# Windowed attention: one 144-column mask-and-exponential per score tile, 32-bit score products for eight units

## The chip, the cores and the metric

The kernel runs on one core of one Trainium2 chip. TensorE (PE in the profile) multiplies; VectorE (DVE), ScalarE (ACT) and GpSimd (POOL) do the rest; SyncE (SP) and ScalarE issue the transfers. The metric is the device time of one execution in microseconds, as the median of three runs.

## What is computed

Three stages follow each other: windowed attention with sink keys, a dense layer with SoLU and layer norm, and a layer of eight experts of which each token uses one. The change touches the attention and the loading of one weight.

```python
# attention, for 4 batches and 8 heads of 768 x 64; n_sink = 4, window = 128
scores = q @ k.T / sqrt(64)
keep = (key < n_sink) | ((0 <= query - key) & (query - key < window))
a = softmax(where(keep, scores, -1e9));  out = a @ v
# dense layer, 3072 tokens: x 512 -> 1024 -> 512
h = x @ w_in;  solu = h * softmax(h);  y = layernorm(solu) * g_ln @ w_out
# experts: e = argmax(y @ w_gate);  result = gate * relu(y @ w1[e]) @ w2[e]
```

## The kernel before

**Attention** works in 32 units of two heads and 384 queries. A unit has six score tiles (three blocks of 128 queries, two heads). A tile has 272 columns: the 128 keys of the block before, 16 sink keys, the 128 keys of the own block (for the first block of a sequence: own keys, sinks, 128 columns that the mask closes). `a_scores` makes the product in PSUM, DVE adds the mask and takes the row's extreme (line 220), ACT takes the exponential and its sum (222). After six tiles DVE adds the two 128-column parts (231: of a query, every key offset lies in one of the two blocks and is masked in the other), POOL scales by the sum (232, and 240 for the sinks). `a_trans` transposes on PE (270), and two masked copies on POOL (274, 276) part the two blocks again. `a_out` multiplies with the values (286, 292), and ACT and DVE split the result into a high and a low part (297, 298), the `xh`, `xl` of the dense layer.

**Scores in two ways.** The first three units (`NATP`) multiply in plain 32-bit: one product per tile on 64 partitions, the two heads on the two halves of the array (line 214). Later units use the faster reduced format, with the operands split into high and low parts (`a_split`): two roundings on ACT (179, 180), two subtractions on POOL (181, 182), nine transfers of SP per unit (187), and then two products of 128 partitions per tile (217, 218).

**Weights.** `w_in` and `w_out` come as 64-bit floats, in 16 chunks of 512 KB. `decode` waits for a transfer that ACT issues (315, three buffers), and works with three DVE operations (319, 321, 326), two of ACT (322, 324) and one of POOL (325); when 325 and 324 are done, the chunk's buffer is free. Its result lies in PSUM. `w_in` then takes one rounding and one subtraction (334, 335). `w_out` takes 363 and 364, a copy to SBUF on ACT (367), and the gate product: four transposes and four small products on PE (343, 351) with a copy between them (345).

**The dense layer** (`moe1`) has 24 tiles of 128 tokens; lines 421 to 423 are the first product (`h`), 491 to 493 the second (`x`). Tiles 3m to 3m+2 need the four units 4m to 4m+3. The experts follow.

**What sets the order.** Each engine runs its instructions in the order of the program. Generators write the work in a fixed interleaving (110 steps of attention with the 16 chunks among them, then both by shares), and a scheduler with its own table of durations reorders that at build time. PSUM has eight banks; attention has three of them (`PA`).

Of the kernel before, what the change touches and what calls it, by code (L numbers as in the profile page):

```python
# [8 lines left out]
F32 = mybir.dt.float32  # L9
F32R = mybir.dt.float32r  # L10
BF16 = mybir.dt.bfloat16
I32 = mybir.dt.int32
U32 = mybir.dt.uint32
AF = mybir.ActivationFunctionType
ALU = mybir.AluOpType
# [10 lines left out]
NEG = -8.0e9  # L26
# [3 lines left out]
NPT, XBUFS, QKB, PKB, VB = 2, 8, 2, 2, 2  # L30
WB, DB, EB, NXR, XGB = 3, 4, 2, 2, 6
PA = 3
NATP = 3
KLV = 2
LA = 2
TE = 18
# [8 lines left out]
E_MIN = struct.unpack("<f", struct.pack("<I", 897 << 20))[0]  # L45


def raw(ap):
    return ap.bitcast(F32)
# [3 lines left out]
def body(ctx, tc, a):  # L53
    nc = tc.nc
    V, A, G, T, SY = nc.vector, nc.scalar, nc.gpsimd, nc.tensor, nc.sync
# [20 lines left out]
    at = a_ctx.enter_context(tc.tile_pool(name="at", bufs=1, side="right"))  # L76

    def ps(name):
        if name in ATT:
            a_ = True  # L80
        elif name in MOE:
            a_ = False
        else:
            flip[0] += 1
            a_ = flip[0] % 8 < PA
        return ps_p.tile([128, 512], F32, tag="psa" if a_ else "psm", name=name, bufs=PA if a_ else 8 - PA)
# [7 lines left out]
                    pattern=[[-1, 128]], channel_multiplier=1)  # L94
# [19 lines left out]
    nsk, win = par[:, 0:1], par[:, 1:2]  # L114


    mkb = at.tile([128, 3, 272], BF16, name="mk")
    mk = at.tile([128, 3, 272], F32, tag="P", name="mkf", bufs=2)
    rel = at.tile([128, 3, 272], F32, tag="P", name="rel", bufs=2)
    mk = at.tile([128, 3, 272], F32, tag="P", name="mkf", bufs=2)  # L120
    kid = const.tile([128, 3, NS], F32, name="kid")
# [15 lines left out]
    def in_win(out, r, tmp):  # L137
# [5 lines left out]
    V.tensor_scalar(out=kid, in0=kid, scalar1=nsk, scalar2=None, op0=ALU.is_lt)  # L143
    V.scalar_tensor_tensor(out=mk[:, :, 128:144], in0=mk[:, :, 128:144], scalar=0.5, in1=kid, op0=ALU.is_lt,
                           op1=ALU.mult)
    V.tensor_scalar(out=mkb, in0=mk, scalar1=-1.0, scalar2=-NEG, op0=ALU.add, op1=ALU.mult)

# [3 lines left out]
    def unit(n):  # L153
        b, c = divmod(n, H)
        return b, c // 4, c % 4

    def a_load(n):
        b, hf, j = unit(n)
        nat = n < NATP
        qd = at.tile([128, 384], F32, tag="qA" if nat else "qd", name="qd", bufs=QKB)  # L160
# [39 lines left out]
    def a_scores(n, mid=()):  # L200

        b, hf, j = unit(n)
        P = at.tile([128, 2, 3, 272], F32, tag="P", name="P", bufs=2)
        mx = at.tile([128, 6], F32, tag="mx", name="mx", bufs=2)
        sm = at.tile([128, 6], F32, tag="sm", name="sm", bufs=2)
        for i in range(3):
            for r in range(2):
                rows = slice(64 * r, 64 * r + 64)
                s = ps("s")
                c0 = 144 * max(3 * hf + i - 1, 0) - KB[hf]  # L210
                qs, ks = slice(128 * i, 128 * i + 128), slice(c0, c0 + 272)
                if n < NATP:
                    q, k = qk_t[n][r]
                    T.matmul(s[:, 0:272], q[rows, qs], k[rows, ks], start=True, stop=True)
                else:
                    q, ql, k = qk_t[n][r]
                    T.matmul(s[:, 0:272], q[:, qs], k[:, ks], start=True, stop=False)  # L217
                    T.matmul(s[:, 0:272], ql[:, qs], k[:, ks], start=False, stop=True)  # L218
                cc = slice(3 * r + i, 3 * r + i + 1)
                V.tensor_tensor_reduce(out=P[:, r, i, :], in0=s[:, 0:272], in1=mkb[:, min(3 * hf + i, 2), :],  # L220
                                       scale=-0.125, scalar=3.0e38, op0=ALU.add, op1=ALU.min, accum_out=mx[:, cc])
                A.activation(out=P[:, r, i, :], in_=P[:, r, i, :], func=AF.Exp, scale=-1.0, bias=mx[:, cc],  # L222
                             accum_out=sm[:, cc])
                yield 0.45 if n < NATP else 0.23
            if i == 1:
                yield from mid
        P = P.rearrange("p r i c -> p (r i) c")
        V.tensor_scalar(out=sm, in0=sm, scalar1=1.0e-9, scalar2=None, op0=ALU.add)
        V.reciprocal(sm, sm)
        pk = at.tile([128, 6, 128], F32, tag="pk", name="pk", bufs=PKB)  # L230
        V.tensor_tensor(out=pk, in0=P[:, :, 0:128], in1=P[:, :, 144:272], op=ALU.add)
        G.tensor_tensor(out=pk, in0=pk, in1=sm.unsqueeze(2).to_broadcast([128, 6, 128]), op=ALU.mult)
        pk_t[n] = pk
        g = n % 2
        if g == 0:
            psk_t[n // 2] = at.tile([128, 3, 4, 2, NS], F32, tag="psk", name="psk")
        psk = psk_t[n // 2].rearrange("p i g a k -> p g i a k")[:, 2 * g:2 * g + 2]
        for r in range(2):
            rs = slice(3 * r, 3 * r + 3)
            G.tensor_tensor(out=psk[:, r], in0=P[:, rs, 128:144].unsqueeze(2).to_broadcast([128, 3, 2, NS]),  # L240
                            in1=sm[:, rs].unsqueeze(2).unsqueeze(3).to_broadcast([128, 3, 2, NS]), op=ALU.mult)
# [66 lines left out]
    def dec_tile(name):  # L308
        return dec_p[0].tile([128, 512], I32, tag="dec", name=name, bufs=DB)

    def decode(src):

        w = dec_p[0].tile([128, 512, 2], I32, tag="w64", name="w64", bufs=WB)
        with tc.issue_after(first_d.ins) if dec_p[0] is at else ExitStack():
            A.dma_start(out=w, in_=src)
        lo, hi = w[:, :, 0], w[:, :, 1]
        t = dec_tile("dec")
        t0 = ps("dt").bitcast(I32)
        V.tensor_scalar(out=t0, in0=hi, scalar1=0x07FFFFFF, scalar2=3, op0=ALU.bitwise_and,
                        op1=ALU.logical_shift_left)  # L320
        V.scalar_tensor_tensor(out=t, in0=hi, scalar=-0x40000000, in1=t0, op0=ALU.bitwise_and, op1=ALU.bitwise_or)
        A.activation(out=lo, in_=lo.bitcast(U32), func=AF.Copy, scale=2.0 ** -29)
        x = ps("dh")
        A.activation(out=x, in_=hi.bitcast(F32), func=AF.Abs)
        G.tensor_tensor(out=t, in0=t, in1=lo, op=ALU.add)
        V.scalar_tensor_tensor(out=x, in0=x, scalar=E_MIN, in1=t.bitcast(F32), op0=ALU.is_ge, op1=ALU.mult)
        return x

    def load_w_in():
        for k in range(4):  # L330
# [7 lines left out]
    def load_w_out():  # L338
        def logits(k, x):

            t = ps("wt")
            for d in range(4):
                T.transpose(t[:, 128 * d:128 * d + 128], x[:, 128 * d:128 * d + 128], ident)
            xt = dec_tile("xt").bitcast(F32).rearrange("p (a b) -> p a b", a=4)
            A.activation(out=xt, in_=t.rearrange("p (a b) -> p a b", a=4), func=AF.Copy)
            return k, xt

        def logits2(k, xt):
            t = ps("wt2")
            for d in range(4):  # L350
                T.matmul(t[:, 0:NE], xt[:, d, :], wg_sb[:, d, :], start=(d == 0), stop=(d == 3))
            wp = t[:, 0:NE]
            gk = g_sb[:, k:k + 1]
            V.tensor_scalar(out=woh[:, k, 0, 256:264], in0=wp, scalar1=gk, scalar2=None, op0=ALU.mult)
            V.scalar_tensor_tensor(out=wol[:, k, 0, 256:264], in0=wp, scalar=gk, in1=raw(woh)[:, k, 0, 256:264],
                                   op0=ALU.mult, op1=ALU.subtract)

        last = last2 = None
        for k in range(8):
            p = decode(a["w_out"].bitcast(I32)[128 * k:128 * k + 128, :])  # L360
            h_ = woh[:, k, :, 0:256]
            p2 = p.rearrange("p (a b) -> p a b", a=2)
            A.activation(out=h_, in_=p2, func=AF.Copy, scale=g_sb[:, k:k + 1])
            V.scalar_tensor_tensor(out=wol[:, k, :, 0:256], in0=p2, scalar=g_sb[:, k:k + 1], in1=raw(h_),
                                   op0=ALU.mult, op1=ALU.subtract)
            x = dec_tile("dec").bitcast(F32)
            A.activation(out=x, in_=p, func=AF.Copy)
            if last2:
                logits2(*last2)
                last2 = None  # L370
            if last:
                last2 = logits(*last)
            last = (k, x)
            yield 1.5
        logits2(*last2)
        logits2(*logits(*last))
# [4 lines left out]
                    channel_multiplier=-1)  # L381
# [704 lines left out]
    def attention():  # L1086
# [34 lines left out]
        for n in range(nu):  # L1121
            if n + 1 < nu:
                a_load(n + 1)
            if n:
                values(n - 1)
            yield from a_scores(n, sinks(n // 2 - 1))
            yield from finish(n, 0)
            if n + 1 < nu:
                a_split(n + 1)
            yield from finish(n, n - 1)  # L1130
# [144 lines left out]
```

## Time and profile before

| | us |
|---|---|
| Median of three runs | 839.44 (838.94 to 843.57) |
| The profiled execution | 844.13, span 842.4 |
| PE busy in the span | 786.0 (93%) |
| DVE, ACT, POOL busy | 495.4, 494.4, 385.4 |
| Mean granted TensorE clock | 0.982 |

The span is the time from the first instruction to the last. Busy shares are averages over stages; what a change is worth is read in the stage that it touches, from the engine on which the others wait there. [...]

### The profile page before, as it was taken

What the parts mean: (1) busy time and instruction counts of PE and PEld (TensorE: products, weight loads), DVE (VectorE), ACT (ScalarE), POOL (GpSimd) and SP (SyncE); (2) the same over time, 40 slices, a digit from 0 to 9 for tenths busy, and PEclk for the clock granted to TensorE, in tenths of its full rate; (3) what the DMA queues carried; (4) which work ended last, traced back from release to release, by engine and by line L of the source; (5) the groups of instructions that cost most, each with busy time, mean ns of one, the idle gap of its engine ahead of it and who ended that gap; (6) DMA issues with size and microseconds to landing.
All of it is one profiled execution on the core that took longest, in us unless ns stands there. A gap on an engine that the chain in (4) does not pass through costs nothing.

```text
span 842.4 us, 14975 instructions
## 1 busy us (share of the span) xinstructions
PE 786.0 (93%) x4906; PEld 682.9 (81%) x4906; DVE 495.4 (59%) x1600; ACT 494.4 (59%) x1232; POOL 385.4 (46%) x418
## 2 busy tenths in 40 slices
PE   4467799999999999999999989989999999999996
PEld 2246678888798888898888879979988898989885
DVE  6877768778777777778765566425313242435431
ACT  4778768777687767776865564225424243435432
POOL 4777763544546454545341020147235253535433
PEclk9978899999999999999999999999999999999999
DMA  8688664547766765557410281087425244436320
GB/s 267 182 217 216 170 162 120 120 102 128 141 162 130 148 120 139 127 147 123 105 39 15 30 239 36 16 261 232 155 89 168 101 141 145 158 125 206 128 101 18
DMA packets 77383, 114.34 MB, mean 136 GB/s; under 512 B 14125, under 2 KB 53485, under 8 KB 77296
## 3 DMA queue, kind: packets, MB, share of 16 engines
q1 hardware_dynamic: 69456, 91.02, 42.7%
q0 software_dynamic: 5248, 13.88, 4.6%
q10 hardware_dynamic: 2592, 8.39, 3.1%
q8 instruction: 41, 0.67, 0.4%
q14 instruction: 46, 0.38, 0.2%
HBM read 72.22 MB, written 13.94 MB: 102 GB/s over the span
## 4 chain that ended last, share of the span: by engine, by line
PE 72%; DMA 12%; issue 5%; DVE 5%; ACT 4%; POOL 1%; SPq 1%; POOLq 0%; ACTq 0%; DVEq 0%
PE ht L774 5%; PE ht L775 5%; PE ht L776 5%; PE x L491 5%; PE y L825 5%; PE y L824 5%; PE y L823 5%; PE x L493 5%; PE x L492 5%; PE h L421 4%; PE h L423 4%; PE h L422 4%; PE av L292 4%; DMA w<-w_out 3%; PE s L217 2%
## 5 line engine op out<-in xcount | busy, mean ns | idle before, releaser
L222 ACT ACTIVATE P<-P,mx 128x272 f32<-128x272 f32 x192 | 98.6, 515 | 32.6 <-DVE mx L220 30.7
L491 PE MATMUL x<-woh,lh 128*128 128x264 f32 (+1 forms) x384 | 112.0, 292 | 0.4 <-DVE ll L474 0.4
L493 PE MATMUL x<-woh,ll 128*128 128x264 f32 (+1 forms) x384 | 110.4, 288 | 0.0
L492 PE MATMUL x<-wol,lh 128*128 128x264 f32 (+1 forms) x384 | 110.0, 287 | 0.0
L695 POOL TENSOR_TENSOR wl<-wst,wh 128x1024 fp32r<-128x1024 f32 x28 | 68.1, 2434 | 63.6 <-ACT wh L689 63.4
L220 DVE CUSTOM_DVE_ANT_0 P<-s,mk 128x272 f32<-128x272 f32 x192 | 79.7, 433 | 29.7 <-PE s L218 27.8
L689 ACT ACTIVATE wh<-wst 128x1024 fp32r<-128x1024 f32 x64 | 67.5, 1058 | 47.8 <-PE ht L775 35.5
L823 PE MATMUL y<-wh,hh 128*128 128x512 f32 x224 | 89.7, 401 | 0.0
L825 PE MATMUL y<-wh,hl 128*128 128x512 f32 x224 | 88.1, 395 | 0.1
L824 PE MATMUL y<-wl,hh 128*128 128x512 f32 x224 | 87.6, 392 | 0.0
L695 DVE TENSOR_TENSOR wl<-wst,wh 128x1024 fp32r<-128x1024 f32 x36 | 53.5, 1494 | 50.7 <-ACT wh L689 50.2
L775 PE MATMUL ht<-xel,wh 128*128 128x288 f32 (+5 forms) x256 | 81.2, 318 | 0.0
L776 PE MATMUL ht<-xeh,wl 128*128 128x288 f32 (+5 forms) x256 | 81.0, 318 | 0.0
L182 POOL TENSOR_TENSOR lA<-qd,qA 128x384 fp32r<-128x384 f32 x29 | 29.3, 1011 | 111.0 <-ACT qA L180 97.5
L774 PE MATMUL ht<-xeh,wh 128*128 128x288 f32 (+5 forms) x256 | 79.7, 318 | 0.0
L421 PE MATMUL h<-wih,bxh 128*128 128x512 f32 x192 | 78.2, 407 | 0.0
L423 PE MATMUL h<-wih,bxl 128*128 128x512 f32 x192 | 77.3, 403 | 0.0
L422 PE MATMUL h<-wil,bxh 128*128 128x512 f32 x192 | 76.3, 397 | 0.0
L491 PEld LDWEIGHTS x<-woh,lh 128*128 128x128 f32 x384 | 73.1, 190 | 1.8 <-issue 0.9
L492 PEld LDWEIGHTS x<-wol,lh 128*128 128x128 f32 x384 | 73.1, 190 | 1.0 <-issue 0.5
L830 ACT ACTIVATE y<-y,gate 128x512 f32<-128x512 f32 x28 | 19.3, 688 | 92.9 <-PE y L825 73.6
L493 PEld LDWEIGHTS x<-woh,ll 128*128 128x128 f32 x384 | 73.1, 190 | 0.2 <-issue 0.2
(240 smaller groups left out, 2095.2 us busy)
## 6 DMA issues: line engine op xcount, KB each, us to landing
wst<-w SPq DMA_DIRECT2D x64, 512.0 KB, 3.8
x_d<-xrow SPq DMA_DIRECT2D x24, 264.0 KB, 7.3
qd<-qT SPq DMA_DIRECT2D x32, 192.0 KB, 2.7
qB<-qA SPq DMA_DIRECT2D x58, 96.0 KB, 2.2
lB<-lA SPq DMA_DIRECT2D x58, 96.0 KB, 2.6
kd<-kx SPq DMA_DIRECT2D x16, 280.0 KB, 3.0
w<-w_in ACTq DMA_DIRECT2D x8, 512.0 KB, 8.9
w<-w_out ACTq DMA_DIRECT2D x8, 512.0 KB, 6.3
```

The lines of the kernel that those rows point to most:

```text
L421: T.matmul(h, xh[k], wih[:, k, cs], start=(k == 0), stop=False)
L423: T.matmul(h, xl[k], wih[:, k, cs], start=False, stop=(k == 3))
L491: T.matmul(p[:, 0:n], lh[:, k, :], woh[:, k, c, 0:n], start=(k == 0), stop=False)
L492: T.matmul(p[:, 0:n], lh[:, k, :], wol[:, k, c, 0:n], start=False, stop=False)
L493: mm = T.matmul(p[:, 0:n], ll[:, k, :], woh[:, k, c, 0:n], start=False, stop=(k == 7))
L695: return (G if c % 2 and r else V).tensor_tensor(out=l_, in0=st_w.pop((r, which, c)), in1=raw(h_), op=ALU.subtract)
L774: T.matmul(o, wh[:, k, fs], xh(k), start=(k == 0), stop=False)
L775: T.matmul(o, wh[:, k, fs], xl(k), start=False, stop=False)
L776: T.matmul(o, wl[:, k, fs], xh(k), start=False, stop=(k == 3))
L823: T.matmul(o, hh[:, k, sl], wh, start=(k == 0), stop=False)
L824: T.matmul(o, hh[:, k, sl], wl, start=False, stop=False)
L825: T.matmul(o, hl[:, k, sl], wh, start=False, stop=(k == 7))
```

## The change

- For every tile but the first block's, DVE copies the own block's scores over the earlier block's where query >= key, in PSUM, under an integer mask (`pick`). The mask addition, the extreme, the exponential and its sum then take 144 columns and not 272; the addition of line 231 is gone. The additive mask is built 144 wide from the larger of the two parts' masks.
- `NATP` goes from 3 to 8: units 3 to 7 are multiplied in plain 32-bit, without `a_split`.
- The last DVE operation of `decode` writes a `w_out` chunk to SBUF, so that the copy of line 367 is gone, and 363 and 364 read SBUF.

```diff
-NATP = 3
+NATP = 8
...
+    V.tensor_tensor(out=mk[:, 1:3, 0:128], in0=mk[:, 1:3, 0:128], in1=mk[:, 1:3, 144:272], op=ALU.max)
+    V.tensor_scalar(out=mkb, in0=mk[:, :, 0:144], scalar1=-1.0, scalar2=-NEG, op0=ALU.add, op1=ALU.mult)
+    pick = at.tile([128, 128], I32, name="pick")
+    G.iota(pick, pattern=[[-1, 128]], base=0, channel_multiplier=1)
+    V.tensor_scalar(out=pick, in0=pick, scalar1=0, scalar2=None, op0=ALU.is_ge)
...
-                V.tensor_tensor_reduce(out=P[:, r, i, :], in0=s[:, 0:272], in1=mkb[:, min(3 * hf + i, 2), :],
+                if 3 * hf + i:
+                    V.copy_predicated(s[:, 0:128], pick, s[:, 144:272])
+                V.tensor_tensor_reduce(out=P[:, r, i, :], in0=s[:, 0:144], in1=mkb[:, min(3 * hf + i, 2), :],
                                        scale=-0.125, scalar=3.0e38, op0=ALU.add, op1=ALU.min, accum_out=mx[:, cc])
...
-        V.tensor_tensor(out=pk, in0=P[:, :, 0:128], in1=P[:, :, 144:272], op=ALU.add)
-        G.tensor_tensor(out=pk, in0=pk, in1=sm.unsqueeze(2).to_broadcast([128, 6, 128]), op=ALU.mult)
+        G.tensor_tensor(out=pk, in0=P[:, :, 0:128], in1=sm.unsqueeze(2).to_broadcast([128, 6, 128]), op=ALU.mult)
...
-        V.scalar_tensor_tensor(out=x, in0=x, scalar=E_MIN, in1=t.bitcast(F32), op0=ALU.is_ge, op1=ALU.mult)
+        y = x if sb is None else sb
+        V.scalar_tensor_tensor(out=y, in0=x, scalar=E_MIN, in1=t.bitcast(F32), op0=ALU.is_ge, op1=ALU.mult)
...
-            p = decode(a["w_out"].bitcast(I32)[128 * k:128 * k + 128, :])
+            x = dec_tile("dec").bitcast(F32)
+            decode(a["w_out"].bitcast(I32)[128 * k:128 * k + 128, :], x)
...
-            x = dec_tile("dec").bitcast(F32)
-            A.activation(out=x, in_=p, func=AF.Copy)
```

The scheduler orders the new program anew. In PE's order, `wt` are the gate products of `w_out` (four transposes, four small products per chunk), `tp` the transposes of a unit, `s` its scores, `h` the dense layer. Before, 84 score products stand ahead of the first `h`, 18 of them plain and 66 split: 8.5 units. This is what stands there:

```order
L217 MATMUL s<-kB,qB 128x272
L218 MATMUL s<-kB,lB 128x272
L351 MATMUL wt_1263<-wg_sb,xt 128x8 x4
L343 MATMUL wt<-ident,dec 128x128 x3
L217 MATMUL s<-kA,qA 128x272
L218 MATMUL s<-kA,lA 128x272
L343 MATMUL wt<-ident,dec 128x128
L421 MATMUL h<-wih,bxh 128x512
```

In the changed program 30 plain score products, five units, stand ahead of it:

```order
L218 MATMUL s<-kd,qd 128x272 x2
L357 MATMUL wt_1169<-wg_sb,xt 128x8 x4
L275 MATMUL tp<-ident,pk 128x128 x3
L349 MATMUL wt<-ident,dec 128x128 x4
L426 MATMUL h<-wih,bxh 128x512
L427 MATMUL h<-wil,bxh 128x512
L428 MATMUL h<-wih,bxl 128x512
```

In both orders the same 28 transposes and 24 small products of `w_out`, seven chunks' worth, stand ahead of the first `h`; it has moved ahead of three and a half units of attention.

On POOL, `dec<-dec,w` is the step of a decode after which its buffer can be refilled. Before, a unit and its split stand between two of them:

```order
L325 TENSOR_TENSOR dec<-dec,w_1095 128x512
L182 TENSOR_TENSOR lA<-qd,qA 128x384
L181 TENSOR_TENSOR kd<-kd,kA 128x416
L274 AFFINE_SELECT pt<-pt 128x6x128
L232 TENSOR_TENSOR pk<-pk,sm 128x768
L240 TENSOR_TENSOR psk<-P,sm 128x3x32 x2
L276 AFFINE_SELECT pt<-pt 128x6x128
L325 TENSOR_TENSOR dec<-dec,w_1159 128x512
```

In the changed program the last two stand side by side, behind two thirds of unit 3's work:

```order
L245 TENSOR_TENSOR psk<-P,sm 128x3x32 x2
L330 TENSOR_TENSOR dec<-dec,w_1067 128x512
L330 TENSOR_TENSOR dec<-dec,w_1156 128x512
L279 AFFINE_SELECT pt<-pt 128x6x128
L237 TENSOR_TENSOR pk<-P,sm 128x768
```

POOL's last decode thus stands ahead of its scaling for unit 4, and before it stood ahead of that for unit 8.

## Rows read from the trace of the kernel before

**Rows 1.** Stretches: length; busy us (count) of PE, PEld, DVE, ACT, POOL; clock; DMA share; GB/s.

```profile
20.00:48.00 28.00, 15.09 (x48) 8.20 (x47) 25.20 (x56) 21.32 (x52) 22.08 (x23) 1.00 0.68 202
60.00:80.00 20.00, 14.98 (x96) 11.92 (x96) 13.86 (x41) 17.28 (x46) 14.26 (x15) 0.83 0.75 198
80.00:100.00 20.00, 15.92 (x103) 13.13 (x100) 15.23 (x48) 17.04 (x49) 15.14 (x17) 0.83 0.73 183
125.00:180.00 55.00, 55.00 (x381) 48.36 (x376) 42.56 (x159) 44.26 (x128) 24.62 (x27) 1.00 0.48 111
```

**Rows 2.** PE's waits from 125 to 482 us: total, times, longest.

```profile
PE s L218 <- DMA lA<-lA: 2.1, 3, 1.2
```

**Rows 3.** PE in order of time: start, us, line, count; a plain product makes two records.

```profile
31.08 1.27 PE L214 MATMUL s<-kd,qd 64*128 64x272 f32 x2 [1.14 <-DVE mx L220]
36.80 1.28 PE L214 MATMUL s<-kd,qd 64*128 64x272 f32 x4
...
70.71 1.06 PE L351 MATMUL wt<-wg_sb,xt 128*128 128x8 f32 x8
71.62 0.63 PE L343 MATMUL wt<-ident,dec 128*128 128x128 f32 x4
72.01 0.37 PE L217 MATMUL s<-kA,qA 128*128 128x272 f32 x1
...
72.35 0.29 PE L217 MATMUL s<-kB,qB 128*128 128x272 f32 x1
72.47 0.29 PE L218 MATMUL s<-kB,lB 128*128 128x272 f32 x1
...
104.89 0.48 PE L421 MATMUL h<-wih,bxh 128*128 128x512 f32 x1
...
137.50 0.39 PE L423 MATMUL h<-wih,bxl 128*128 128x512 f32 x1
137.73 0.82 PE L270 MATMUL tp<-ident,pk 128*128 128x128 f32 x6
138.30 0.60 PE L286 MATMUL av<-skt,vsk 128*128 128x384 f32 x2
138.83 1.30 PE L292 MATMUL av<-pt,vd 128*64 128x256 f32 x12
140.06 0.39 PE L491 MATMUL x<-woh,lh 128*128 128x264 f32 x1
```

**Rows 4.** Refills of decode buffers: the fifth's issue; the last's, behind POOL's step.

```profile
53.89 0.36 ACTq L315 DMA_DIRECT2D w<-w_out  x1
...
79.02 1.29 POOL L325 TENSOR_TENSOR dec<-dec,w 128x512 int32<-128x512 int32 x1
...
80.34 0.33 ACTq L315 DMA_DIRECT2D w<-w_out  x1
```

**Rows 5.** All refills for w_out (x8): ns of an issue, first and last start.

```profile
L315 ACTq DMA_DIRECT2D w<-w_out x8: 334/335/371, 34.1 to 80.3; - x8
```

**Rows 6.** Groups from 0 to 125 us: busy us, mean ns, idle before.

```profile
L222 ACT ACTIVATE P<-P,mx 128x272 f32<-128x272 f32 x60 | 30.8, 515 | 8.7 <-DVE mx L220 7.5 <-POOL vsk L249 1.2
L322 ACT ACTIVATE w<-w 128x512 int32<-128x512 uint32 x16 | 10.8, 675 | 17.7 <-DMA w<-w_in 9.8 <-DMA w<-w_out 8.0
L231 DVE TENSOR_TENSOR pk<-P 128x768 f32<-128x768 f32 x10 | 10.6, 1061 | 0.0
L367 ACT ACTIVATE dec<-dh 128x512 f32<-128x512 f32 x8 | 4.7, 585 | 1.3 <-DVE wol L364 1.3
L180 ACT ACTIVATE qA<-qd 128x384 fp32r<-128x384 f32 x9 | 4.6, 515 | 0.0
```

**Rows 7.** DVE in order of time: start, us, line; the second starts when the first's reading ends.

```profile
12.38 0.43 DVE L220 CUSTOM_DVE_ANT_0 P<-s,mk 128x272 f32<-128x272 f32 x1
...
12.74 0.43 DVE L220 CUSTOM_DVE_ANT_0 P<-s,mk 128x272 f32<-128x272 f32 x1
```

**Rows 8.** ACT's exponentials from 60 to 100 us, as in rows 6.

```profile
L222 ACT ACTIVATE P<-P,mx 128x272 f32<-128x272 f32 x24 | 12.3, 517 | 1.0 <-DVE mx L220 1.0
```

More of the change, by code (lines that the diff above doesn't have):

```diff
@@ L114, in body @@
     nsk, win = par[:, 0:1], par[:, 1:2]
-    mkb = at.tile([128, 3, 272], BF16, name="mk")
+    mkb = at.tile([128, 3, 144], BF16, name="mk")
     mk = at.tile([128, 3, 272], F32, tag="P", name="mkf", bufs=2)
@@ L145, in body @@
                            op1=ALU.mult)
-    V.tensor_scalar(out=mkb, in0=mk, scalar1=-1.0, scalar2=-NEG, op0=ALU.add, op1=ALU.mult)
+    V.tensor_tensor(out=mk[:, 1:3, 0:128], in0=mk[:, 1:3, 0:128], in1=mk[:, 1:3, 144:272], op=ALU.max)
[3 more added lines that the diff above has]
+    V.tensor_scalar(out=pick, in0=pick, scalar1=0, scalar2=None, op0=ALU.is_ge)
     ld_t, qk_t, v_t, vk_t, pk_t, vsk_t, psk_t, skt_t, pt_t, x_t = {}, {}, {}, {}, {}, {}, {}, {}, {}, {}
@@ L202, in a_scores @@
         b, hf, j = unit(n)
-        P = at.tile([128, 2, 3, 272], F32, tag="P", name="P", bufs=2)
+        P = at.tile([128, 2, 3, 144], F32, tag="P", name="P", bufs=2)
         mx = at.tile([128, 6], F32, tag="mx", name="mx", bufs=2)
@@ L309, in dec_tile, with decode @@
         return dec_p[0].tile([128, 512], I32, tag="dec", name=name, bufs=DB)
-    def decode(src):
+    def decode(src, sb=None):
         w = dec_p[0].tile([128, 512, 2], I32, tag="w64", name="w64", bufs=WB)
@@ L325, in decode @@
         G.tensor_tensor(out=t, in0=t, in1=lo, op=ALU.add)
-        V.scalar_tensor_tensor(out=x, in0=x, scalar=E_MIN, in1=t.bitcast(F32), op0=ALU.is_ge, op1=ALU.mult)
-        return x
+        y = x if sb is None else sb
+        V.scalar_tensor_tensor(out=y, in0=x, scalar=E_MIN, in1=t.bitcast(F32), op0=ALU.is_ge, op1=ALU.mult)
+        return y
     def load_w_in():
@@ L359, in load_w_out @@
         for k in range(8):
-            p = decode(a["w_out"].bitcast(I32)[128 * k:128 * k + 128, :])
+            x = dec_tile("dec").bitcast(F32)
+            decode(a["w_out"].bitcast(I32)[128 * k:128 * k + 128, :], x)
             h_ = woh[:, k, :, 0:256]
-            p2 = p.rearrange("p (a b) -> p a b", a=2)
+            p2 = x.rearrange("p (a b) -> p a b", a=2)
             A.activation(out=h_, in_=p2, func=AF.Copy, scale=g_sb[:, k:k + 1])
```

## The prediction

> **What bounds the kernel now.** I read the table of stretches first. From 125 to 180 us PE is busy for the whole 55 us at a clock of 1.00 [rows 1], and the list of PE's waits from 125 to 482 us holds one entry, 2.1 us for a transfer [rows 2]. There the time is PE's, DVE is busy for 42.6 of 55 us and ACT for 44.3, and what the change takes from these two is worth nothing by itself. Ahead of 125 us no engine is full. From 60 to 100 us ACT is busy 34.3 of 40 us, DVE 29.1, POOL 29.4, and PE's 30.9 us are at a clock of 0.83 [rows 1]: engines that wait for each other in turn, ACT the busiest. A change can gain only in PE's lost time there, so I measure that.
>
> PE's work at full clock, from the timeline of PE: one score product of a split tile 0.125 us (72.35 to 72.47), so 0.25 per tile; the four transposes and eight small products of a `w_out` chunk 0.39 + 0.91 (71.62 to 72.01; 70.71 to 71.62); one `h` 0.23 (137.50 to 137.73); six transposes of a unit 0.57; its value products 0.53 + 1.23 (to 140.06), 0.1 each of the twelve [rows 3]. A plain product is dearer, by how much at full load no row says: two of them, on the two halves of the array, took 1.28 us where one took 1.27 [rows 3], so a pair costs what one costs, with idle time on either side. Less the 0.16 that a split product runs past the start of the next (0.29 − 0.125), a pair costs 1.12 at most; at least I put the 0.5 of the two split tiles that it replaces. The sums below count it at 0.5, and the surplus stands as a term of its own.
>
> With these prices I added up what PE had finished by 125 us: scores 15.0 us (9 plain pairs 4.5, 84 split products 10.5), transposes 5.1, sinks 1.2, values 15.3, eight chunks of gate products 10.4, 31 `h` 7.1, in all 54.1. PE had lost 125 − 54.1 = 70.9 us. At the first `h`, at 104.89 [rows 3], it had finished 37.3 and lost 67.6; so the loss ends almost there, and 3.3 us come in the 20 behind it. **The first `h` is what decides**: from there PE has work of its own.
>
> **Decode pace.** What holds `h` back is the order. PE runs in order, and seven chunks of gate products stand ahead of the first `h`. A refill of a decode buffer is issued behind POOL's step three chunks earlier: 79.02 + 1.29 us, and ACT's issue at 80.34 [rows 4]. The eight refills run from 34.1 to 80.3 [rows 5], 6.6 us each, and the last three steps, from 53.89 on, 8.8 us each [rows 4]. The order paces them: between two decode steps of POOL stood a whole unit of attention.
>
> **The change, part by part.**
>
> *First `h` moved.* Ahead of it 30 plain score products stand (15 pairs) and not 84 split and plain ones, 21 transposes and not 54, with the same 28 transposes and 24 small products. At full clock PE has 21.8 us ahead of it: 7.5 + 2.0 + 0.6 (sinks) + 3.5 (values) + 8.2 (gate products). Three and a half units of attention, and all their work on ACT and DVE, now stand behind it.
>
> *144 columns.* Line 220 starts 0.36 us apart at 272 columns [rows 7]; I take some 0.08 of it as fixed (the accumulator is read behind each) and the rest as columns (an estimate), so that 144 columns take 0.23. The copy under a mask, PSUM to PSUM, is in no row. It has 128 columns: between 0.13 (the same fixed part and little else) and 0.36 (as long as the wider reduction [rows 7]); I take 0.20, nearest the narrow reduction. A unit has five copies on average (1.0), six narrower reductions (6 × 0.13 = 0.78 less) and no line 231, whose row says 1.06 for the instruction [rows 6] and some 0.87 for its share of the engine: DVE −0.67 us per unit, at 0.36 about +0.1. ACT's exponential goes from 515 ns [rows 6] to about 0.41, −0.64 per unit. POOL's scaling reads the same 768 columns: nothing.
>
> Each copy is a step in the chain from product to exponential that no row has; a score bank is held 0.20 + 0.23 us and not 0.36. Ahead of 125 us five units pay 0.07 six times, 2 us at most, beside other work; behind it DVE has 12 of 55 us free [rows 1], so nothing.
>
> [...]
>
> *Units 3 to 7 plain.* Their split is gone: two roundings on ACT (515 ns each [rows 6]), two subtractions on POOL, nine transfers of SP per unit, with the waits for them. On PE 15 pairs take the place of split tiles. Six of them run ahead of the new first `h`, where PE waits anyway; nine (units 5 to 7) run behind it, where PE's time counts: at 0.5 a pair nothing, at 1.12 it is 9 × 0.62 = 5.6 us. I take 0.7, nearer the split, since behind the first `h` PE has dense work around it: +2 us.
>
> *`w_out` to SBUF.* ACT is rid of eight copies of 585 ns [rows 6] in the chain from the decode to the transposes. Lines 363 and 364 read SBUF: taken as equal.
>
> **The time of the first `h`.** ACT and DVE price the way to it. From 60 to 100 us, with 24 exponentials, four units [rows 8], and some four decodes (refills 8.8 us apart), ACT was busy 34.3 us, so 8.6 for a unit and a chunk, DVE 7.3 [rows 1]. One of a decode's two ACT operations takes 0.675 [rows 6]; splitting the sums by the kinds of instruction, ACT has about 3.2 per chunk and 5.4 per unit, DVE 2.7 and 4.5 (estimates). In the new kernel a chunk costs ACT 2.6 (without the copy) and a unit 3.7 (without roundings, with narrower exponentials), DVE 2.7 and 3.8. I anchor at 48 us, where three units' scores and two chunks were through: from 20 to 48 us DVE was busy 25.2 of 28 [rows 1], and what the change adds there (decodes that moved ahead) I set against what it takes. From there two units and six chunks are left: ACT 6 × 2.6 + 2 × 3.7 = 23.0 us, DVE 23.8, PE some 15 at full clock. At ACT's share of 60 to 100 us, 0.86 [rows 1], 23.8 take 27.7: **first `h` at 76 us**. Bounds: 72 without gaps, 85 with PE at half clock throughout and the old waits on it.
>
> The loss up to there is 76 − 21.8 = 54.2. The three and a half units now behind it leave PE about 35 us of its own against DVE's 29 and ACT's 27, and 3.3 us lost per 20 becomes 5.8 per 35: 60.0 in all, 10.9 less than 70.9. Off go 2 for the plain pairs and 1 for a new risk: attention then runs some one unit ahead of the dense layer and not three, so at the seven further half-batches a late unit can stop PE (one whole chain uncovered, transposes to `h`, is about 5 us; covered, nothing; I bound the sum at 0 to 7). The gain is **7.9 us**. The profiled execution took 844.13 us, 4.7 above the median of 839.44; the difference carries over, as it is made of work and waits ahead of 125 us: 839.4 − 7.9 = 831.5, given as 832.
>
> **Rivals.**
> 1. *Larger gain.* Without gaps the first `h` is at 72 and the loss behind it 2, since ACT and DVE have less to do there: 72 − 21.8 + 2 = 52.2, 18.7 less than 70.9; with the 2 for the pairs 16.7: 823. For it: the chain of a chunk is shorter by a copy. Against: ACT's share from 60 to 100 us is 0.86 with the same kinds of work [rows 1].
> 2. *No change.* The decodes keep up only in part, the first `h` is at 83.9 (the point where the 7.9 us are used up) or a little before or behind, 839; or the pairs cost 1.12, 831.5 + 3.6 = 835. Range 835 to 843. For it: the 1.28 us row, and the copy's upper price (0.16 × 5 × 5 units = 4 us of DVE ahead of the first `h`).
> 3. *Slower: PE stands before the gate products.* If refills stay 8.8 us apart from 53.89 on [rows 4], because ACT's issue still waits behind other ACT work, the seventh chunk's gate products, and so the first `h`, come at about 101 us, hardly ahead of the old 104.89. PE in order can't pass them, and the attention it used to do meanwhile now stands behind: 101 − 21.8 + 5.8 = 85.0 lost, 14.1 more, +3 for pairs and late units: 856.5. It decides from 83.9 us on. For it: each refill waits for ACT and POOL, three chunks earlier. Against: POOL's last decode step has moved ahead of four units' scaling.
>
> **How the numbers follow.** Half a per cent (4.2 us: 835.2 and 843.6) is about what a measurement of this kernel can tell from no change. The forecast, 827 to 835, has 0.45, the larger gain 0.20, no change 0.22, slower 0.13. Faster is the first two, 0.65. The range holds 821 (rival 1 with 2 us of luck) to 843 (the upper end of rival 2) and leaves out rival 3 and a little below.
>
> **What would show it.** In the profile after: the first `h` at about 76 us, `w_out` refills done by about 65, PE full from about 115, no roundings before unit 8, the copy at about 0.2 us between starts, PE's waits from 125 to 482 us still a few us. The forecast is wrong if the first `h` comes behind 83 us, or if PE shows waits at the half-batches that add up to over 7 us, or if plain products near full clock take over 0.7 us a pair.

## The result: slower by 0.6%, where a gain was forecast

| | before | after |
|---|---|---|
| Median of 12 runs, us | 840.71 | 844.63 |
| Ratio | 1 | 1.0063 (1.0034 to 1.0092) |
| The profiled execution, us | 844.13 | 849.64 |
| Its span, us | 842.4 | 847.9 |

A second measurement of the same kernel gave 1.0042 (1.0009 to 1.0076). The forecast was 832. Here and below, medians are over all runs of a kernel, while the ratios leave out a few runs in which the chip was in a slower state (without its one such run, of 1355 us, the median of natp3_no_copy is 822.1).

The stretches of the profile after, with the columns of [rows 1]:

```profile
20.00:48.00 28.00, 17.50 (x68) 9.96 (x68) 26.68 (x73) 22.34 (x56) 20.42 (x21) 1.00 0.61 206
60.00:80.00 20.00, 18.33 (x84) 13.39 (x86) 13.41 (x49) 10.28 (x28) 8.35 (x10) 0.67 0.13 39
80.00:100.00 20.00, 20.00 (x98) 13.77 (x98) 7.03 (x30) 5.60 (x18) 3.76 (x5) 1.00 0.11 38
100.00:125.00 25.00, 20.55 (x100) 13.38 (x100) 16.91 (x76) 19.57 (x62) 12.59 (x16) 0.80 0.48 120
125.00:180.00 55.00, 54.53 (x393) 47.99 (x392) 37.24 (x163) 38.07 (x120) 27.10 (x32) 1.00 0.55 127
```

From 80 to 100 us PE is now full at full clock, where it was at 15.92 of 20 and 0.83. But DVE is busy 7.03 us there (15.23 before), ACT 5.60 (17.04): the dense layer has PE, and attention stands. Then, from 100 to 125 us, PE falls to 20.55 of 25 at 0.80.

The decodes and the first `h`, from the source view of line 320 (an issue's ns, first and last start) and the timeline of PE, as [rows 5] and [rows 3] show them of the kernel before:

```profile
L320 ACTq DMA_DIRECT2D w<-w_out x8: 334/334/339, 29.8 to 55.0; - x8
```

```profile
70.69 0.78 PE L426 MATMUL h<-wih,bxh 128*128 128x512 f32 x1
...
78.77 0.72 PE L218 MATMUL s<-kd,qd 64*128 64x272 f32 x2
79.43 0.50 PE L428 MATMUL h<-wih,bxl 128*128 128x512 f32 x1
79.85 0.73 PE L218 MATMUL s<-kd,qd 64*128 64x272 f32 x4
80.51 1.06 PE L357 MATMUL wt<-wg_sb,xt 128*128 128x8 f32 x8
```

The first `h` starts at 70.69 and not at 104.89, and the last refill is issued at 55.0 and not at 80.3. A pair of plain products takes 0.66 (79.85 to 80.51), and so does one alone (78.77 to 79.43), at a granted clock of 1.00 from 77 to 82 us.

PE's waits from 125 to 482 us, where [rows 2] had one entry, 2.1 us:

```profile
PE av L291 <- DVE mx L226: 1.6, 3, 0.6
PE lt L475 <- ACT e L460: 1.5, 3, 0.6
PE s L222 <- DMA lA<-lA: 1.4, 1, 1.4
PE s L221 <- issue: 1.1, 1, 1.1
PE s L221 <- ACT pt L276: 0.7, 1, 0.7
PE x L496 <- ACT h L451: 0.3, 1, 0.3
```

They are spread over attention and the dense layer, 6.6 us in all. So the stage up to 125 us gained about what was forecast, and later stages gave it back. For all kernels below I worked out PE's lost time as the prediction does: the time up to a moment, less PE's finished products at the prediction's prices (0.66 for a plain pair; the rest at the pitch from one start to the next where PE is full). It is an estimate; a profiled execution can also lie some us off its kernel's median (from 5.0 below, lead1, to 5.0 above, the changed kernel). All of PE's work comes to 741.2 us with three plain units and to 743.6 with eight. One execution of each kernel was profiled; two of the same kernel (before twice, after twice) differ by up to 3 us in a column.

| kernel | median, us | ratio to before (interval) | lost by 125 us | 125 to 480 | behind 480 |
|---|---|---|---|---|---|
| before, and again | 840.7 | 1 | 71.4, 74.2 | 12.9, 11.5 | 16.9, 17.5 |
| after, and again | 844.6, 846.0 | 1.0063, 1.0042 | 64.4, 62.7 | 20.8, 19.0 | 19.1, 19.8 |
| natp8_only | 833.7 | 0.990 (0.987 to 0.994) | 63.4 | 11.5 | 16.0 |
| sbuf_only | 829.9 | 0.985 (0.981 to 0.989) | 59.7 | 15.1 | 13.7 |
| copy144_only | 851.3 | 1.012 (1.007 to 1.016) | 69.4 | 20.2 | 17.5 |
| sbuf_natp8 | 838.8 | 0.998 (0.994 to 1.001) | 57.2 | 18.5 | 16.2 |
| sbuf_natp5 | 830.8 | 0.989 (0.986 to 0.992) | 59.1 | 13.1 | 15.8 |
| copy144_natp8 | 841.1 | 1.001 (0.999 to 1.004) | 54.1 | 20.3 | 20.1 |
| changed_natp3 | 836.8 | 0.994 (0.991 to 0.996) | 56.4 | 18.7 | 13.9 |
| natp3_no_copy | 822.9 | 0.980 (0.976 to 0.984) | 55.1 | 11.7 | 11.9 |
| natp3_free_copy | 837.0 | 0.995 (0.992 to 0.998) | 58.1 | 16.0 | 19.2 |
| natp3_copy16 | 836.4 | 0.996 (0.993 to 0.999) | 59.5 | 17.8 | 18.9 |
| natp3_late16 | 829.8 | 0.990 (0.986 to 0.993) | 55.4 | 11.5 | 19.1 |
| lead1 | 845.9 | 1.005 (1.002 to 1.008) | 59.9 | 23.1 | 12.6 |
| dbl_copy | 874.2 | 1.038 (1.033 to 1.043) | 72.6 | 36.8 | 18.5 |
| lead1_dbl_copy | 879.0 | 1.043 (1.038 to 1.047) | 73.0 | 46.2 | 15.4 |

The first `h` of natp8_only, of copy144_natp8 and of natp3_no_copy, for the reading of the early stage below:

```profile
101.68 0.48 PE L421 MATMUL h<-wih,bxh 128*128 128x512 f32 x1
```

```profile
82.05 0.48 PE L426 MATMUL h<-wih,bxh 128*128 128x512 f32 x1
```

```profile
83.38 0.78 PE L424 MATMUL h<-wih,bxh 128*128 128x512 f32 x1
```

### The profile page after: what moved, and what is told of

The parts are those of the page before. It is cut to its first block, busy times and chain, and to the rows that moved or that the text cites. A ratio compares the mean times of both kernels' runs of the same rounds, so it can differ in the third digit from the quotient of the medians.

```text
span 847.9 us, 15142 instructions
## 1 busy us (share of the span) xinstructions
PE 794.8 (94%) x4906; PEld 680.9 (80%) x4906; DVE 471.7 (56%) x1730; ACT 467.4 (55%) x1214; POOL 368.2 (43%) x409
## 4 chain that ended last, share of the span: by engine, by line
PE 68%; DMA 11%; issue 8%; DVE 7%; ACT 3%; POOL 2%; SPq 0%; POOLq 0%; ACTq 0%; DVEq 0%
DMA id_d<-tok_i,si 6%; PE y L830 5%; PE y L828 5%; PE y L829 5%; PE ht L779 5%; PE ht L780 5%; PE ht L781 5%; PE h L427 4%; PE h L426 4%; PE av L297 4%; PE h L428 4%; PE x L496 4%; PE x L498 4%; PE x L497 4%; PE s L221 2%
## 5 line engine op out<-in xcount | busy, mean ns | idle before, releaser
L228 ACT ACTIVATE P<-P,mx 128x144 f32<-128x144 f32 x192 | 78.5, 410 | 47.1 <-DVE mx L226 42.4
L700 DVE TENSOR_TENSOR wl<-wst,wh 128x1024 fp32r<-128x1024 f32 x36 | 55.6, 1552 | 50.4 <-ACT wh L694 48.6
L428 PE MATMUL h<-wih,bxl 128*128 128x512 f32 x192 | 75.5, 404 | 0.0
L225 DVE COPY_PREDICATED s<-pick,s 128x128 f32<-128x128 int32 x160 | 45.1, 290 | 52.7 <-PE s L222 33.1
L186 POOL TENSOR_TENSOR lA<-qd,qA 128x384 fp32r<-128x384 f32 x24 | 24.3, 1013 | 106.6 <-ACT qA L184 93.1
```

Of the source, the lines that this page charges most:

```text
L700: return (G if c % 2 and r else V).tensor_tensor(out=l_, in0=st_w.pop((r, which, c)), in1=raw(h_), op=ALU.subtract)
```

## Experiments on where the gain went

**Theory 1: the dense layer runs too close behind attention.** The scheduler moved it ahead in the whole program. In PE's order 80, 114, 152, 186 and 216 of the value products, those of the sinks included (nine per unit on average), stood ahead of the second to sixth half-batch before; now 62, 88, 124, 160 and 196, two to three units less. Measured beside each other: the changed kernel again, the same with attention's old lead, and both with each copy made twice.

> The changed kernel unaltered, for a second profile beside the others. Accounts: at 240 us PE's lost time is some 8 us less than before, at 450 us as much as before. Theory 1 (dense layer runs two units of attention earlier than before, so PE stands for late units) and rival 2 (the copy lengthens each unit's chain) both expect 1.003 to 1.009 of before and waits of PE of 5 to 9 us in all from 125 to 480 us. Rival 3 (chance: the one profile was an unlucky execution): waits of 2 us there, and the give-back gone.

It measured 1.0042: the loss is no accident of one run. In the two profiles of the changed kernel PE had lost 7 to 11.5 us less than before at 125 us, and about as much or somewhat less at 480 (81.7 and 85.2; before 84.3 and 85.7).

```diff
+LEAD = 1
...
-            T.matmul(h, xh[k], wih[:, k, cs], start=(k == 0), stop=False)
+            with tc.issue_after(av_i[min(4 * (t // 3) + 3 + LEAD, 31)].ins) if av_i and k == 0 and t > 2 else ExitStack():
+                T.matmul(h, xh[k], wih[:, k, cs], start=(k == 0), stop=False)
...
```

> The changed kernel; from the second half-batch on the first product of each dense tile is ordered behind unit 4m+4's value products, so that attention leads as in the kernel before (80, 114, 152 value products ahead of the half-batches, not 62, 88, 124). Theory 1: early gain kept (first h near 71 us, lost time at 150 us as in the changed kernel or up to 3 us more), waits from 125 to 480 us down to 2 or 3 us, 6 to 8 us off the changed kernel: 836 to 838.5, ratio to before 0.994 to 0.998. Rival 2 (copy): 843 to 846, waits as in the changed kernel. Rival 3: within 2 us of the changed kernel.

845.9: the lead of before, and the time of the changed kernel. Theory 1 falls as it stood. The lead alone gives nothing back; PE lost 23.1 us from 125 to 480 even so. Its waits there, 7.3 us in all, are others than those of the changed kernel; two of the five kinds:

```profile
PE tp L276 <- DVE mx L227: 2.0, 5, 0.7
PE s L222 <- DVE mx L227: 1.9, 5, 0.7
```

`mx` is what the reduction of a score tile gives; with it a bank of attention comes free, and the kernel places `tp` and `s` in these banks.

```diff
                     V.copy_predicated(s[:, 0:128], pick, s[:, 144:272])
+                    V.copy_predicated(s[:, 0:128], pick, s[:, 144:272])
```

> The changed kernel with each masked copy made twice (the second writes the same values): DVE gets 160 more instructions of 0.29 us, 1.5 us per unit, and each tile's chain one more step. Theory 1: early stage 1 to 3 us later, the waits behind 125 us grow by 1 to 3 us: 846 to 850. Rival 2: the give-back doubles, 851 to 855.

> Both: attention's lead of before, each copy twice. Theory 1: the lead covers the longer chain, so 0 to 3 us over the run with the lead alone (837 to 841). Rival 2: 7 us or more over it, whatever the lead (844 to 853).

874.2 and 879.0, some 28 and 33 us more than with one copy: far more than either theory said, and not less with the lead. 160 further instructions at 0.2 us are 32 us of DVE, in a program whose DVE is busy for 56% of the time; PE lost 8 to 10 us more by 125 us and 16 to 18 more from 125 to 480. The copies had a price although DVE had free time.

**The parts one by one.** N is NATP = 8, C the copies with 144 columns, S the decode of `w_out` to SBUF. Each of these kernels is the one before with some of the parts (or the changed one without the others); the lines of C are those from `mkb` to `pk` in the diff of the change, and of N and S:

```diff
-NATP = 3
+NATP = 8
...
-            p = decode(a["w_out"].bitcast(I32)[128 * k:128 * k + 128, :])
+            x = dec_tile("dec").bitcast(F32)
+            decode(a["w_out"].bitcast(I32)[128 * k:128 * k + 128, :], x)
...
```

> The kernel before with NATP = 8 and nothing else: the order keeps attention's long lead (80, 114, 152 value products ahead of the half-batches), no copies. Theory 2 (the copies under the mask give the gain back: a tile's chain has one more step on DVE, which runs in order): nothing here gives back, so the early stage loses some us less (splits gone) and PE has 2.4 us more work: ratio 0.992 to 1.000. Rival 4 (the dearer plain products are what makes the change slower): 1.002 to 1.006.

> The kernel before with the copies and the 144 columns and nothing else (NATP 3, decode through PSUM). Theory 2: slower than before behind 125 us by some 6 us, little gained ahead of it: 1.003 to 1.010. Rival 4: 0.992 to 1.000, since the exponential and DVE's addition are shorter.

> The kernel before with w_out decoded to SBUF and nothing else: the scheduler moves the dense layer ahead here too (48 score products ahead of the first h, 160 value products ahead of the fifth half-batch), without copies and with three plain units. Theory 2: the early gain stays, 0.990 to 0.997. Theory 1 in what is left of it (a short lead costs): 0.998 to 1.004.

> The changed kernel with NATP back at 3: copies, 144 columns and decode to SBUF. Theory 2: still slower than before, 1.001 to 1.006, as the copies stay. Rival 4: 2.4 us less work for PE than in the changed kernel and the early gain kept: 0.994 to 1.000.

> The kernel before with w_out decoded to SBUF and NATP = 8, without copies: the missing corner between these two parts. From the single parts (0.985 and 0.990 of before): if the plain units cost only when the copies are there (theory 2), the gains add in part, 820 to 828. Theory 6 (plain units and an early dense layer get in each other's way: h runs out while PE stands for the plain units' chains, 100 to 125 us, with or without copies): 832 to 840, and PE's lost time grows by 8 us or more between 100 and 125 us.

> The changed kernel with w_out decoded through PSUM as before: copies, 144 columns and eight plain units. By the parts alone (+9 for the copies, -8 for the plain units): 840 to 845 if they add (theory 2). Theory 6: 846 to 854, as in the changed kernel the plain units find no use with an early dense layer.

> The kernel before unaltered, for a second profile: all accounts expect PE's lost time within 4 us of the first profile's (71 at 125 us, 84 at 480 us), the difference being stretches of lower clock.

With the table's ratios the corners are: none 1, N 0.990, C 1.012, S 0.985, CN 1.001, CS 0.994, NS 0.998, all three 1.004 to 1.006. Two rules hold in all of them. **C costs 0.7 to 1.2%** in whatever company (none to C, N to CN, S to CS, NS to all), 6 to 10 us. And **N and S don't add**: N alone gains 1.0% and S alone 1.5%, but with S there N costs 1.0 to 1.3%. It takes both to make the change slower: without N it is 0.6% faster than before (changed_natp3). Theory 2 (the copies) and theory 6 (the interference of N and S) stand for the signs. Rival 4 falls as it stood, since natp8_only is 8.6 us faster than before although its PE has 2.4 us more work; but its range held for changed_natp3 (0.994, where theory 2 had 1.001 to 1.006), and beside S the plain units do cost. Theory 2 had the sizes of three single corners a little off: 0.990 for 0.992 to 1.000, 1.012 for 1.003 to 1.010, 0.985 for 0.990 to 0.997. Theory 6 missed copy144_natp8: 841.1 for 846 to 854.

**How the copies cost.** The kernel with C and S was the base (changed_natp3). Without the copies, and with the rest of C as it was, it took 822.9, 13.9 us less (12 by the ratios). That is the price of the copies by themselves. Against sbuf_only (829.9), which has the 272 columns, natp3_no_copy is 7 us faster, with intervals that overlap; so the narrower columns seem to earn about half of what the copies cost, and C's 6 to 10 us is the difference.

```diff
-                if 3 * hf + i:
-                    V.copy_predicated(s[:, 0:128], pick, s[:, 144:272])
```

> The changed kernel with NATP 3 and without the copies: the own block's scores are left out of the result (144 columns are masked, reduced and exponentiated as in the change). Theory 2 (the copies give the gain back): PE loses 11 to 15 us between 125 and 480 us, not 19 as with them, and the time is 822 to 830. Rival 5 (it is the scheduler's other order that costs, not the copies): 834 to 838 as with the copies.

The prices to be told apart are the step in a tile's chain (2a), the time on DVE (2b) and the bank (5b). `z` is a spare tile in SBUF.

```diff
-                    V.copy_predicated(s[:, 0:128], pick, s[:, 144:272])
+                    V.copy_predicated(z, pick, s[:, 144:272])
```

> The changed kernel with NATP 3, each masked copy written to a spare SBUF tile that nothing reads (so the own block's scores are left out of the result): as many DVE instructions of the same size, but the reduction no longer waits for the copy. With the copies this kernel took 836.8 us, without them 822.9. Theory 2a (the step in the chain of a tile, product, copy, reduction, is what costs): 822 to 828. Rival 2b (the instructions' time on DVE costs, 160 x 0.2 us): 832 to 838.

```diff
-                    V.copy_predicated(s[:, 0:128], pick, s[:, 144:272])
+                    V.copy_predicated(s[:, 0:16], pick[:, 0:16], s[:, 144:160])
```

> The changed kernel with NATP 3, each masked copy cut to 16 of its 128 columns (the other 112 columns of the own block are left out of the result): the step in the chain stays, its columns go. Theory 2a with the step's fixed part: 830 to 837. Rival 2b: 823 to 827, as the time on DVE falls to less than half.

837.0 and 836.4: neither the dependence nor the length is the price by itself. But a step in the tile's chain is left in both. DVE of natp3_free_copy, and then of natp3_copy16:

```profile
133.66 0.30 DVE L226 COPY_PREDICATED z<-pick,s 128x128 f32<-128x128 int32 x1 [0.45 <-PE s L222]
133.87 0.30 DVE L227 CUSTOM_DVE_ANT_0 P<-s,mk 128x144 f32<-128x144 f32 x1
```

```profile
134.15 0.18 DVE L225 COPY_PREDICATED s<-pick,s 128x16 f32<-128x16 int32 x1 [0.43 <-PE s L222]
134.37 0.31 DVE L226 CUSTOM_DVE_ANT_0 P<-s,mk 128x144 f32<-128x144 f32 x1
```

The reduction starts 0.21 us behind a copy that it doesn't read, and 0.22 behind the short one that it does. So natp3_free_copy, of which theory 2a expected 822 to 828, did not take the step away, and natp3_copy16 came out as 2a expected of a step with a fixed price (830 to 837): theory 2a is not excluded. Both kernels keep one more thing: the copy stands ahead of the reduction on DVE, as the first instruction there that needs PE's product. Theory 2c says that this is what costs. The next kernel makes the 16-column copy behind the reduction:

```diff
...
-                    V.copy_predicated(s[:, 0:128], pick, s[:, 144:272])
...
+                    with tc.issue_after(red.ins):
+                        V.copy_predicated(z, pick[:, 0:16], s[:, 144:160])
```

> The changed kernel with NATP 3; in place of each masked copy one of 16 columns to a spare tile stands behind the tile's reduction instead of ahead of it (the own block's scores are left out of the result). As many DVE instructions as with 16-column copies ahead of the reduction (836.4 us); without any it was 822.9. Theory 2c (DVE stands at each copy until PE's product is there, and what is queued behind it comes later): 822 to 828. Rival 5c (any 160 more instructions of DVE, or the order that the scheduler makes with them, cost this): 832 to 838.

829.8, between the two expectations: 6.6 us of the 13.5 are back. By the ratios, 0.990 for 0.994 to 0.996 in the three kernels with the copy ahead, it is 4 to 5 us, and the intervals overlap a little. DVE's longest waits for score products from 125 to 482 us (in all, times, longest), of natp3_no_copy, of changed_natp3, of natp3_copy16, of natp3_late16 and of lead1:

```profile
DVE P L224 <- PE s L222: 23.0, 41, 2.0
```

```profile
DVE s L225 <- PE s L222: 46.8, 47, 3.1
DVE P L226 <- PE s L222: 7.7, 9, 2.7
```

```profile
DVE s L225 <- PE s L222: 43.0, 48, 2.9
DVE P L226 <- PE s L222: 5.4, 5, 2.4
DVE P L226 <- PE s L221: 5.0, 5, 2.5
```

```profile
DVE P L224 <- PE s L222: 24.4, 34, 2.2
DVE P L224 <- PE s L221: 5.1, 3, 3.8
```

```profile
DVE s L226 <- PE s L223: 15.2, 27, 1.9
DVE P L227 <- PE s L222: 5.0, 3, 2.8
```

With a copy ahead of the reduction, of 128 columns or of 16, DVE stands for PE's score products for 53 to 55 us, in natp3_no_copy and natp3_late16 for 23 to 30. But this alone is not the price. DVE's idle time as a whole is much the same in these four, 119 to 125 of the 355 us from 125 to 480; what changes is what it stands for. And lead1, with the copies ahead of the reduction, stands for 20 us only, where the changed kernel stands for 51, and is no faster. PE's own waits in that stretch, all of them, of changed_natp3 and of natp3_late16:

```profile
PE rk L521 <- DVE L L505: 1.6, 1, 1.6
PE av L291 <- DVE sc L449: 1.2, 2, 0.8
PE h L426 <- DVE ll L479: 0.8, 2, 0.6
PE lt L475 <- ACT e L460: 0.6, 1, 0.6
PE tp L275 <- DVE sc L459: 0.6, 1, 0.6
PE tp L275 <- DVE mx L226: 0.3, 1, 0.3
```

```profile
PE x L498 <- ACT h L453: 1.0, 3, 0.4
```

Of the former 4.5 us of 5.1 are ended by DVE, and 4.2 by its work for the dense layer (`L`, `sc`, `ll`), not by scores. In natp3_free_copy, of the same time, DVE ends none of PE's waits there (`lA` 2.1, `e` 1.0), and PE lost 16.0 us all the same. PE lost 11.5 us from 125 to 480 with the copy behind, 11.7 with none, 16.0 to 18.7 with it ahead. So the place of the copy counts for some 4 to 7 of its 12 to 14 us, by one kernel and at the edge of what the intervals tell. How the cost runs is not shown: through work that stands on DVE behind a waiting copy, through a step of some 0.2 us in the tile's chain, which natp3_late16 takes away as well, or through the bank that is held meanwhile. The waits are from one execution each, they differ among kernels that pay the same, and the scheduler laid out each kernel anew. What natp3_late16 still has over natp3_no_copy lies behind 480 us in its profile, 7.2 us, around one wait of PE for the experts' first gather:

```profile
PE xt L744 <- DMA xg<-x_d,idx_i: 3.8, 2, 3.6
```

natp3_no_copy had no such wait; most kernels here have one, of 1 to 5 us, the one before among them. Why it comes and goes I did not find.

**The bank.**

```diff
-PA = 3
+PA = 4
```

> The changed kernel with NATP 3 and four PSUM banks for attention (PA = 4, the dense layer has four left of five). Rival 5b (the copy holds a score bank longer, and PE waits for a bank): the copies' price of 12 to 13 us against the same kernel without copies falls to 0 to 5 us beside the next run. Theory 2a: the price stays 7 us or more beside the next run.

> The kernel before with w_out decoded to SBUF, no copies, and four banks for attention: the measure for the run ahead of it. All accounts: 825 to 840; the difference to natp3_four_banks is what counts (with three banks it was 829.9 against 836.8, 7 us).

844.0 (1.0037, 1.0005 to 1.0069) with the copies and 849.0 (1.0063, 1.002 to 1.011) without, where the runs lie in two groups, 839.7 to 841.3 and 847.9 and above. With four banks the copies' price isn't there, as 5b expected; but both are slower than with three, and their PE stood 5.5 us with copies and 8.1 without for one kind of transfer (`lA`), which cost 2.0 without copies and with three banks. Two so different orders don't settle it: the bank stays possible as a part of the price.

**Eight plain units and the early dense layer.** changed_natp3 and the changed kernel differ by N alone; here is changed_natp3 where attention stood still in the changed kernel:

```profile
60.00:80.00 20.00, 19.25 (x97) 17.17 (x98) 18.34 (x51) 12.79 (x32) 14.24 (x14) 0.59 0.69 176
80.00:100.00 20.00, 19.82 (x117) 16.45 (x117) 13.53 (x59) 12.40 (x41) 8.64 (x10) 1.00 0.39 108
100.00:125.00 25.00, 24.30 (x177) 21.10 (x176) 17.98 (x83) 21.92 (x68) 11.48 (x15) 1.00 0.55 143
```

From 80 to 100 us DVE works 13.53 us (7.03 with N) and ACT 12.40 (5.60); from 100 to 125 PE is at 24.30 of 25 with full clock (20.55 and 0.80 with N). DVE's longest group of waits from 70 to 100 us in the changed kernel, and in changed_natp3:

```profile
DVE s L225 <- PE s L218: 13.6, 7, 5.6
```

```profile
DVE s L225 <- PE s L222: 3.2, 4, 2.2
```

In the changed kernel PE's order puts long runs of `h` between single plain products; DVE waits up to 5.6 us for one, and attention behind it. At 100 us `h` gives way to attention whose chains have not started. PE stands idle for 4.5 of the next 25 us, and works the rest at a granted clock of 0.80. It lost 12.3 and 10.6 us between 100 and 125 us (two executions); changed_natp3 lost 2.0. An early `h` with eight plain units is not enough for this: copy144_natp8 has both, with its first `h` at 82.05 and not at 70.69, and PE is busy for all of the 25 us there at a clock of 1.00. Eight of the plain products between 75 and 101 us also stand alone, at 0.66 each.

> The kernel before with w_out decoded to SBUF and five plain units: between three (829.9 us) and eight (838.8). If each plain unit beyond the third costs its dearer products and a part of the waits: 831 to 836. If the cost comes with the last of them only (units 6 and 7, needed at the second half-batch): 827 to 831.

830.8, with the interval of sbuf_only's ratio overlapping: two more plain units cost about nothing, and the cost comes with the last three. In sbuf_natp8, without copies, it doesn't show at the place that was expected: PE lost 1.6 us from 100 to 125 us, and 7.8 from 180 to 240, where its clock was 0.94 and where it waited 3.5 us for the transfers of split units:

```profile
PE s L218 <- DMA lA<-lA: 2.0, 1, 2.0
PE s L217 <- DMA qA<-qA: 1.5, 1, 1.5
```

So the interference is shown with the copies and without them. Its way is read from the traces of the changed kernel beside changed_natp3, and no run changes this order alone; for sbuf_natp8 it stays open.

**A faster version** fell out of this: sbuf_only, the kernel before with the third part of the change alone, at 829.9 us (0.985), beats both kernels; sbuf_natp5, at 830.8, can't be told from it.

## Point by point

- *What bounds the kernel; the first `h` decides.* Right that PE's lost time ahead of 125 us can be won; that the first `h` decides it is not borne out. The first `h` was forecast for 76 us and came at 70.7. The lost time at 125 us fell by 7 to 11.5 us, where 10.9 were forecast. But natp8_only had lost as little by 125 us (63.4, for 64.4 and 62.7) with its first `h` hardly moved, at 101.68, and natp3_no_copy only 55.1 with its first `h` at 83.38. In the changed kernel the gain came in another shape than forecast: only 52.1 us were lost by 100 us, where the forecast had 54.2 by 76, and then 10.6 to 12.3 us between 100 and 125, where 5.8 were set for 35 us. The 5.8 were scaled from a stretch in which attention still led.
- *Where the gain comes from.* The forecast took it as the sum of the moved decodes, the splits and the shorter exponentials. One part was enough: w_out's decode to SBUF, "ACT is rid of eight copies", lets the scheduler start `h` at 80.9 us and gains 12.4 us by itself. The plain units gain 8.6 by themselves; with both in place 1.7 are left, which the interval does not tell from none. So this sum of parts failed as well: beside the other two parts the plain units were to help, at a price of 2 us of PE, and they cost 8 to 9 us (836.8 without them, 844.6 and 846.0 with them). In the profiles, which lie further apart than the medians, it shows from 100 to 125 us and behind 480 us (13.9 lost there without them, 19.1 and 19.8 with them). Without the plain units the change would have been faster, 0.994.
- *144 columns.* The sizes were right. The reduction starts every 0.22 to 0.23 us (0.23), two copies stand 0.2 apart (0.20), the exponential takes 409 ns (0.41). But the number of copies had a price that these sizes don't give: 160 more took 28 to 30 us more (dbl_copy), and shorter ones were no cheaper (natp3_copy16).
- **The step that failed:** "behind it DVE has 12 of 55 us free [rows 1], so nothing". The price of the copies behind 125 us was taken from DVE's free time and put at nothing. The runs showed 12 to 14 us for the copies by themselves, and 6 to 10 us for C in each of four pairs. In three of these pairs PE's lost time from 125 to 480 us grew with C (12.9 and 11.5 to 20.2, 11.5 to 20.3, 15.1 to 18.7), and so it did with the copies alone (11.7 to 18.7). In the fourth, from sbuf_natp8 to the changed kernel, it grew ahead of 125 us (57.2 to 64.4 and 62.7) and by only 0.5 to 2.3 us behind it. DVE's free time did not cover them, and 16 columns cost as much as 128. Their place ahead of the reduction seems to be a third to a half of the price. The prediction did name the chain and the bank, and priced them by durations alone; which of these, or the work queued on DVE, carries the price stays open.
- *Late units at the half-batches*, a term of 1 us with bounds of 0 to 7. The loss from 125 to 480 us grew by 6 to 9. The bound held for most of it, the value did not; and the lead, to which the prediction put it, isn't the cause, as lead1 shows. Behind 480 us, which the prediction left out, PE lost some 2 us more.
- *Plain pairs*, +2 us for nine pairs: 0.66 a pair against 0.7 taken; PE's whole work grew by 2.4 us for 15 pairs, with up to 2.6 more (8 × 0.33) for those that stood alone.
- *The slower rival* (decodes that stay 8.8 us apart) was wrong: the eight refills are 3.6 us apart. The change came out slower for a reason that no rival had.

## What to carry to other kernels

Where engines run in order and one is full, don't price an added instruction by the free time of its own engine. Here 160 copies on an engine that was idle for a third of the stretch cost 12 to 14 us, as much with 16 columns as with 128, and less behind the reduction than ahead of it: add or move the instruction alone and measure. Measure the parts of a change alone and together before believing a sum; two that shorten the same stage can cost each other, and here the least conspicuous part alone was the best kernel that computes the whole result. When an order is made anew, read in the stretches which engines go quiet while the bound one is full: in the changed kernel such a quiet (DVE busy for 7.03 of 20 us) stood ahead of the stall (PE idle for 4.5 of the next 25).

## What the runs showed of the hardware

Behind a masked copy of 128 columns an instruction of DVE that doesn't read what the copy wrote started 0.19 us later (the changed kernel, the first two lines), and a reduction that reads it 0.33 later (changed_natp3, the last three):

```profile
17.44 0.28 DVE L225 COPY_PREDICATED s<-pick,s 128x128 f32<-128x128 int32 x1
17.63 0.68 DVE L341 TENSOR_TENSOR wil<-dh,wih 128x512 fp32r<-128x512 f32 x1
...
163.46 0.30 DVE L225 COPY_PREDICATED s<-pick,s 128x128 f32<-128x128 int32 x1 [1.56 <-PE s L222]
163.79 0.31 DVE L226 CUSTOM_DVE_ANT_0 P<-s,mk 128x144 f32<-128x144 f32 x1
164.02 0.08 DVE L226 DVE_READ_ACCUMULATOR2_ANT mx<- 128x1 f32 x1
```

So a copy and its own reduction hold a bank for at least 0.33 + 0.23 us (163.46 to 163.79, 163.79 to 164.02) where 0.43 were counted. The read of the accumulator takes 0.08 us here, and in the kernel before:

```profile
12.74 0.08 DVE L220 DVE_READ_ACCUMULATOR2_ANT mx<- 128x1 f32 x1
```

It starts together with the second reduction of [rows 7], 0.36 us behind the start of the first; that the first's reading ends there is not shown. From 0.36 us at 272 columns and 0.22 to 0.23 at 144, the part that doesn't go with the columns comes to 0.06 to 0.08 us (an estimate), where the prediction took 0.08.

And PE's clock is a part of the loss from 100 to 125 us: it was granted 0.80 there in the changed kernel, where PE was idle for 4.5 us, and 1.00 in changed_natp3, where it was idle for 0.7. Idle time alone doesn't tell the clock: in the kernel before 0.50 was granted from 85 to 90 us, with PE idle for 0.1 us.
